# Gated linear attention and a cosine router: causal scores without their empty quarter, all masks on GpSimd

## The chip, the cores and the metric

The kernel runs on one core of a Trainium2 chip. The metric is the device time of one execution in microseconds (us). The core has a matrix engine (TensorE, in the profile PE, with its weight loads as PEld), a vector engine (VectorE, DVE), a scalar engine (ScalarE, ACT), a general engine (GpSimd, POOL) and an engine that issues transfers (SyncE, SP). Each runs its own instructions in order, and they wait for each other through semaphores. Sixteen DMA engines move data.

## The reference

Two blocks follow each other. The first is a recurrence with 4 batches, 8 heads, 768 positions and a head size of 48; its output is the input of a router with 8 experts of 1024 hidden units:

```python
for t in range(S):
    state = alpha[:, :, t, :, None] * state + np.einsum('bhd,bhe->bhde', k[:, :, t], v[:, :, t])
    y[:, :, t] = np.einsum('bhd,bhde->bhe', q[:, :, t], state)
...
x = np.ascontiguousarray(attn_out.transpose(0, 2, 1, 3)).reshape(B * S, H * D)
...
logits = xn @ en.T / tau
expert_idx = np.argmax(logits, axis=1)
...
    h = np.maximum(x[mask] @ w1[e], 0.0)
    out[mask] = gate_w[mask, None] * (h @ w2[e])
```

All data are fp32.

## The kernel before

**Stages.** The recurrence is computed in 24 chunks (`NS`) of 128 positions, six to a batch. Within a chunk it is an attention with decays: scores of all keys with all queries, masked so that a key acts on its own and later positions only, times `v`, and to it the queries times the state carried from the chunk before. Afterwards a routed expert stage runs over blocks of 128 tokens. The change touches the attention stage alone.

**A chunk.** Eight heads make four pairs (`NP = 4`); a pair's two heads, padded to 64, fill the 128 partitions. `decays` turns `alpha`, `k` and `q` on TensorE (`pa`, `pk`, `pq`), makes on VectorE the scan `r` and the keys `kr = pk * r` (L484). `queries` copies `pq` to `qc` on ScalarE; `decay_queries` makes the scan `a` on VectorE and the queries `qs = qc * a` on GpSimd (L510). `scores` makes for each pair, each half of the keys (64) and each head `hh` one product of 64 keys and 128 queries, each on a quarter of the array (64 rows by 64 columns), into one PSUM tile `sc` per `hh`. The mask is put on by VectorE for `hh = 0`, as a product with a triangle (L577); for `hh = 1` ScalarE copies the scores to SBUF (L578) and GpSimd's `affine_select` clears them (L579). `mix_states` puts queries times `dec` (the state with its decay, made on GpSimd, L535) into `pyx`; `mix_chunk` adds eight products of 128 keys and 128 queries (L617). `update` makes `pd` from the keys and `v`, and VectorE the new `state` (L560). `rows` turns `y` back to rows with the logits (`px`, `lg`, `x`).

**Order.** The loop over steps is a hand-written pipeline: step `s` makes decays and queries of chunk `s`, scores and masks of `s - 1`, `y` of `s - 2`, rows of `s - 3`. `in_turn` and `behind` order instructions behind named earlier ones (`issue_after`), so that each engine's queue has the order of the program:

```python
            if 0 <= s - 1 < NS:
                decay_state(s - 1)

                with in_turn(), tc.issue_after(st[s]["a_scan"].ins) if s < NS else ExitStack():
                    scores(s - 1)
```

**Transfers.** `load` issues the loads of a chunk on SyncE, two chunks ahead; four buffers each hold `alpha`, `k`, `q`, and five `v` (L455). When the tokens of a group of chunks have been routed (`choose`, `place`), their rows go to an HBM table `xs` by expert: `to_rows` (L311) is an indirect transfer of 128 rows of 393 floats, issued by GpSimd, here called a send. In the steps from the ninth on GpSimd issues one or two of them, behind the `qs` of the step. `fetch_early` (L181) loads the first rows of an expert on SyncE once the sends of the first 16 chunks have landed, and the first expert's weights (L141, L144) are issued behind it. In 15 steps GpSimd also clears a part of a later buffer (L784), and it keeps the running counts of the experts (L340).

Of the kernel before, what the change touches and what calls it, by code (L numbers as in the profile page):

```python
# [9 lines left out]
FP32 = mybir.dt.float32  # L10
I32 = mybir.dt.int32
AF = mybir.ActivationFunctionType
ALU = mybir.AluOpType
# [14 lines left out]
def kernel(  # L28
# [12 lines left out]
    nc = tc.nc  # L41
    B, H, S, D = q.shape
    E, DM = expert_emb.shape
    F = w1.shape[2]
    P = 128
    DP = 64
    NP = H // 2
    NCH = S // P
    N = B * S
    NS = N // P  # L50
# [4 lines left out]
    HALF = P // 2  # L55
# [18 lines left out]
    consts = ctx.enter_context(tc.tile_pool(name="consts", bufs=1))  # L74
# [1 line left out]

    ident = consts.tile([P, P], FP32)
    make_identity(nc, ident)
    causal = consts.tile([P, 1, P], FP32)
    earlier = consts.tile([P, P], FP32)  # L80
    ones = consts.tile([P, P], FP32)
    cols_i = consts.tile([P, E], I32)
# [4 lines left out]
    part = consts.tile([P, 1], FP32)  # L87
# [102 lines left out]
    def mm(*args, **kwargs):  # L190
        last["pe"] = nc.tensor.matmul(*args, **kwargs)  # L191
# [4 lines left out]
    def in_turn():  # L196
        return tc.issue_after(last["pe"].ins) if last else ExitStack()


    with ExitStack() as c1:  # L200
        keep = c1.enter_context(tc.tile_pool(name="keep", bufs=1))
        work = c1.enter_context(tc.tile_pool(name="work", bufs=2))
        ps_tr = c1.enter_context(tc.tile_pool(name="ps_tr", bufs=3, space=PSUM))
        ps_sc = c1.enter_context(tc.tile_pool(name="ps_sc", bufs=1, space=PSUM))
# [4 lines left out]
        NBUF, NBV = 4, 5  # L209
# [2 lines left out]
        kt_s = [keep.tile([P, H, DP], FP32, name=f"kt{i}") for i in range(NBUF)]  # L212
        vt_s = [keep.tile([P, H, DP], FP32, name=f"vt{i}") for i in range(NBV)]

        NR = 3
        r_s = [keep.tile([P, NP * P], FP32, name=f"r{i}") for i in range(NR)]

# [3 lines left out]
        def fixed_parts():  # L221
            for i in range(NBUF):
                nc.gpsimd.memset(at_s[i][:, :, D:DP], 1.0)

                nc.gpsimd.memset(at_s[i][0:1], 0.0)
                nc.vector.memset(kt_s[i][:, :, D:DP], 0.0)
                nc.vector.memset(qt_s[i][:, :, D:DP], 0.0)
                if i == 0:
                    nc.gpsimd.memset(inr, 0.0)
                    for p in range(NP - 1):  # L230
                        nc.gpsimd.memset(inr[:, p * P + P - 1 : (p + 1) * P], 1.0)
                    for j in range(NR):
                        nc.vector.memset(r_s[j][:, NP * P - 1 :], 1.0)
                if i < 2:
                    nc.vector.memset(ini_s[i], 0.0)
            make_upper_triangular(nc, causal[:, 0], val=1.0, diag=True)
            for i in range(NBV):
                nc.vector.memset(vt_s[i][:, :, D:DP], 0.0)

        chunk_of = "b h (c p) d -> b c p h d"  # L240
        a_r, q_r, k_r, v_r = (t.rearrange(chunk_of, p=P) for t in (alpha, q, k, v))
# [149 lines left out]
        def counts(n):  # L391
# [32 lines left out]
            nc.vector.tensor_tensor(used, bc(r, shp, 2), bc(starts, shp, 1), ALU.is_gt)  # L424
            return nc.vector.tensor_copy(used_i, used[0:1])

        st = [dict() for _ in range(NS)]
        carried = {}

        def turned(t, name):  # L430
            pt = ps_tr.tile([P, NP * P], FP32, tag="tr", name=name)
            with in_turn():
                for p in range(NP):
                    tr(
                        pt[:, p * P : (p + 1) * P],
                        t[:, 2 * p : 2 * p + 2].rearrange("p h d -> p (h d)"),
                        ident,
                    )
            return pt
# [4 lines left out]
        def load(s):  # L444

            if s < NS:
                b, c = divmod(s, NCH)
                i = s % NBUF
                for p0, p1 in ((1, AROW), (AROW, P)):
                    nc.sync.dma_start(out=at_s[i][p0:p1, :, 0:D], in_=a_r[b, c, p0:p1])  # L450
                nc.sync.dma_start(out=kt_s[i][:, :, 0:D], in_=k_r[b, c])
                nc.sync.dma_start(out=qt_s[i][:, :, 0:D], in_=q_r[b, c])
            if s > 0:
                b, c = divmod(s - 1, NCH)
                return nc.sync.dma_start(out=vt_s[(s - 1) % NBV][:, :, 0:D], in_=v_r[b, c])  # L455

        def behind(s):

# [5 lines left out]
        def decays(s):  # L464

            d = st[s]
            i = s % NBUF
            L = NP * P
            pa = turned(at_s[i], "pa")
            r = r_s[s % NR]
            nc.vector.tensor_tensor_scan(  # L477
                r[:, L - 2 :: -1], pa[:, L - 1 : 0 : -1], inr[:, L - 2 :: -1],
                1.0, ALU.mult, ALU.add,
            )  # L480
            pk = turned(kt_s[i], "pk")
            d["kr"] = kr = work.tile([P, NP, P], FP32, name="kr", bufs=3)
            krf = kr.rearrange("p n t -> p (n t)")
            nc.vector.tensor_tensor(krf, pk, r, ALU.mult)  # L484
            d["pq"] = turned(qt_s[i], "pq")
            d["a"] = pa, r

# [7 lines left out]
        def decay_queries(s):  # L495
            c = s % NCH
            d = st[s]
            L = NP * P
            pa, r = d["a"]
            rv = r.rearrange("p (n t) -> p n t", t=P)  # L500
            ini = ini_s[s % 2]
            nc.vector.reciprocal(
                ini.rearrange("p (n t) -> p n t", t=P)[:, :, 0:1], rv[:, :, 0:1]
            )
            a = work.tile([P, L], FP32, name="a")
            d["a_scan"] = by_dve = nc.vector.tensor_tensor_scan(  # L506
                a, pa, ini, 0.0, ALU.mult, ALU.add
            )
            d["qs"] = qs = work.tile([P, NP, P], FP32, name="qs", bufs=4)
            by_pool = nc.gpsimd.tensor_tensor(  # L510
                qs.rearrange("p n t -> p (n t)"), d["qc"], a, ALU.mult
            )
            if c > 0:
                d["end"] = end = work.tile([P, NP, 1], FP32, name="end", bufs=3)
                nc.gpsimd.tensor_tensor(end, rv[:, :, 0:1], al0[:, :, s : s + 1], ALU.mult)
            d["last"] = by_dve, by_pool
# [45 lines left out]
        def scores(s):  # L562

            d = st[s]
            kr, qs = d["kr"], d["qs"]
            d["sm"] = sm = [work.tile([P, NP, P], FP32, name=f"sm{hh}") for hh in range(2)]
            sc = [ps_sc.tile([P, NP, P], FP32, name=f"sc{hh}") for hh in range(2)]
            for p in range(NP):
                for i in range(2):
                    to = slice(i * HALF, (i + 1) * HALF)  # L570
                    for hh in range(2):
                        sl = slice(DP * hh, DP * hh + DP)
                        mm(
                            sc[hh][to, p], lhsT=kr[sl, p, to], rhs=qs[sl, p],
                            start=True, stop=True, skip_group_check=True,
                        )
            nc.vector.tensor_tensor(sm[0], sc[0], causal.to_broadcast([P, NP, P]), ALU.mult)  # L577
            nc.scalar.copy(sm[1], sc[1])  # L578
            d["masked"] = nc.gpsimd.affine_select(  # L579
                out=sm[1], in_=sm[1], pattern=[[0, NP], [1, P]], base=0,  # L580
                channel_multiplier=-1, compare_op=ALU.is_ge, fill=0.0,
            )

# [22 lines left out]
        def mix_chunk(s):  # L608

            d = st[s]  # L610
            pyx, sm, vt = d["pyx"], d["sm"], vt_s[s % NBV]
            d["yT"] = yT = [work.tile([P, NQ, P], FP32, name=f"ycols{hh}") for hh in range(2)]
            for hh in range(2):
                for p in range(NP):
                    q, to = p // 2, DP * (p % 2)
                    mm(
                        pyx[hh][to : to + DP, q * P : (q + 1) * P],  # L617
                        lhsT=vt[:, 2 * p + hh], rhs=sm[hh][:, p],
                        start=("dec" not in d and q == 0), stop=True, skip_group_check=True,
                    )  # L620
                nc.scalar.copy(yT[hh].rearrange("p q t -> p (q t)"), pyx[hh][:, 0:YX])

        def rows(s):
# [92 lines left out]
        for s in range(NS + 3):  # L716
# [9 lines left out]
            if s < NS:  # L726
                decays(s)
# [9 lines left out]
            if s < NS:  # L737
                queries(s, copied)
                decay_queries(s)
            if 0 <= s - 1 < NS:  # L740
                decay_state(s - 1)

                with in_turn(), tc.issue_after(st[s]["a_scan"].ins) if s < NS else ExitStack():
                    scores(s - 1)
            if s == 0:
                with behind(s), in_turn():
                    prepare_first(a0)
                with behind(s):
                    prepare_logits()
# [7 lines left out]
                    mix_chunk(s - 2)  # L757
            if 0 <= s - 1 < NS:

                with in_turn(), tc.issue_after(st[s]["a_scan"].ins) if s < NS else ExitStack():  # L760
                    update(s - 1)
            if 0 < s < NS and s % NCH == 0:

# [17 lines left out]
            if 4 <= s < 4 + NXG * (NC + 1):  # L781
                i, t = divmod(s - 4, NC + 1)
# [6 lines left out]
            if s >= NS:  # L789
                n = placing(s)  # L790
# [14 lines left out]
            for r in rows_of(s):  # L805
                g = group_of[r]
# [578 lines left out]
```

## Time and profile before

| what | value |
|---|---|
| median of 14 executions | 416.43 us (415.88 to 418.13) |
| the profiled execution | 418.62 us, its span 416.7 us |
| busy in the span: PE, PEld, DVE, ACT, POOL | 398.3, 353.6, 287.7, 195.0, 221.2 us |
| attention stage in the span | up to about 155 us |
| DMA packets of under 512 bytes | 102,287 of 119,379 |

How to read it: busy time is summed over the whole span, and the stages have different limits; the windows and the timeline show a stage by itself. "L579" is line 579 of the kernel before. In lines of the waits the three numbers are the total in us, how often, and the longest. In lines of the timeline the numbers are start and duration in us, and in brackets the idle time of the engine just before it and what ended it. A fp32 product appears as two records on PE.

### The profile page before, as it was taken

The page shows a single profiled execution, that of the slowest core. Times are in us where ns is not written, and L with a number is a line of the kernel's source. Part 1 is how long each engine was busy: PE and PEld are TensorE (multiplying, and loading weights), DVE is VectorE, ACT ScalarE, POOL GpSimd, SP SyncE. Part 2 cuts the span into 40 slices and gives each one's busy share as a digit, 9 for nine tenths or more (in the row PEclk, how much of TensorE's full clock was granted, in tenths as well). Part 3 has the DMA queues.
Part 4 walks back from the last instruction along what each step waited for, and adds up shares of the span by engine and source line. Part 5 has one row for each costly group of instructions (what it writes and reads, how often), then busy time and mean ns, then how long its engine had stood idle before and what let it go on. Part 6 is the DMA issues. An engine that isn't in the chain of part 4 may idle for free. (4 is left out here: it accounts for less than half of the span.)

```text
span 416.7 us, 12552 instructions
## 1 busy us (share of the span) xinstructions
PE 398.3 (96%) x4954; PEld 353.6 (85%) x4954; DVE 287.7 (69%) x634; ACT 195.0 (47%) x481; POOL 221.2 (53%) x288
## 2 busy tenths in 40 slices
PE   7999999999989899999999999999999999999994
PEld 6789979888879677678979989889979989979974
DVE  7898979699799515882596696692595379487530
ACT  4455544455435424553653643732651472662320
POOL 7546577767665436831762843932671482682001
PEclk9999999999999999999999999999999999999998
DMA  9999999999994893595703805604701900101001
GB/s 138 159 163 156 155 207 179 198 183 187 198 174 113 295 349 112 150 359 171 263 16 117 297 18 184 220 19 147 260 19 39 339 28 19 41 0 36 21 16 43
DMA packets 119379, 60.28 MB, mean 145 GB/s; under 512 B 102287, under 2 KB 113816, under 8 KB 119312
## 3 DMA queue, kind: packets, MB, share of 16 engines
q1 hardware_dynamic: 115208, 49.14, 49.5%
q0 software_dynamic: 3728, 10.16, 6.9%
q8 instruction: 46, 0.75, 0.8%
q14 instruction: 21, 0.17, 0.1%
q10 hardware_dynamic: 376, 0.05, 0.1%
HBM read 49.69 MB, written 11.45 MB: 147 GB/s over the span
## 5 line engine op out<-in xcount | busy, mean ns | idle before, releaser
L852 POOL DMA_INDIRECT out_dram<-y,sx x25 | 24.6, 982 | 103.4 <-DVE y L1161 42.3
L982 DVE TENSOR_TENSOR hT<-pq,hT 128x512 f32<-128x512 f32 x63 | 43.6, 692 | 46.2 <-PE pq L1082 44.4
L1082 PE MATMUL pq<-xT_m,w_m 128*128 128x128 f32 x560 | 67.2, 275 | 0.0
L1082 PEld LDWEIGHTS pq<-xT_m,w_m 128*128 128x128 f32 x560 | 64.7, 192 | 0.3 <-issue 0.3
L510 POOL TENSOR_TENSOR qs<-qc,a 128x512 f32<-128x512 f32 x24 | 30.6, 1276 | 37.0 <-DVE a L506 22.9
L1034 POOL TENSOR_TENSOR w_m<-w_m,w 128x512 f32<-128x512 f32 x30 | 43.2, 1446 | 1.4
L965 PE MATMUL pyo<-w,hT 128*128 128x384 f32 x128 | 42.6, 486 | 0.0
L1082 PE MATMUL pq<-xT_m,w 128*128 128x128 f32 x280 | 38.4, 277 | 0.6
L1082 PEld LDWEIGHTS pq<-xT_m,w 128*128 128x128 f32 x280 | 34.9, 192 | 2.1 <-issue 1.8
L987 ACT ACTIVATE hT<-hT 128x512 f32<-128x512 f32 x35 | 22.1, 631 | 31.2 <-DVE hT L982 31.2
L965 PEld LDWEIGHTS pyo<-w,hT 128*128 128x128 f32 x128 | 23.7, 190 | 14.8
L477 DVE TENSOR_TENSOR_SCAN r<-pa,inr 128x511 f32<-128x511 f32 x24 | 29.2, 1215 | 6.1 <-PE pa L194 5.9
L191 PE MATMUL sc<-qs,kr 64*64 64x128 f32 x768 | 29.6, 273 | 3.8 <-issue 3.8
L311 POOL DMA_INDIRECT xs<-x,dest x24 | 24.2, 1009 | 13.3 <-DVE x L653 8.4
L506 DVE TENSOR_TENSOR_SCAN a<-pa,ini 128x512 f32<-128x512 f32 x24 | 29.3, 1223 | 1.0
L1154 PE MATMUL pq<-w_m,hT_m 128*128 128x192 f32 x168 | 28.4, 326 | 0.0
L191 PEld LDWEIGHTS sc<-qs,kr 64*64 64x64 f32 x768 | 22.8, 133 | 6.2 <-issue 6.0
L1154 PEld LDWEIGHTS pq<-w_m,hT_m 128*128 128x128 f32 x168 | 27.5, 190 | 0.0
L191 PE MATMUL pyx<-sm,vt 128*64 128x128 f32 x384 | 26.3, 279 | 0.0
L649 ACT COPY lg<-pyx 128x32 f32<-128x32 f32 x24 | 4.4, 185 | 44.5 <-PE px L191 38.3
L191 PEld LDWEIGHTS pyx<-sm,vt 128*64 128x64 f32 x384 | 20.5, 136 | 4.3 <-issue 3.6
L1034 POOL TENSOR_TENSOR w_m<-w 128x512 f32<-128x512 f32 x12 | 15.3, 1274 | 15.9 <-PE pq L1082 15.9
(229 smaller groups left out, 917.7 us busy)
## 6 DMA issues: line engine op xcount, KB each, us to landing
w<-in_moe_w_dram SPq DMA_DIRECT2D x16, 1536.0 KB
kt<-in_k_dram SPq DMA_DIRECT2D x24, 192.0 KB
qt<-in_q_dram SPq DMA_DIRECT2D x24, 192.0 KB
vt<-in_v_dram SPq DMA_DIRECT2D x24, 192.0 KB
xg<-xs SPq DMA_DIRECT2D x22, 196.5 KB
at<-in_alpha_dram SPq DMA_DIRECT2D x24, 168.0 KB
xg<-xs SPq DMA_DIRECT2D x8, 98.2 KB
at<-in_alpha_dram SPq DMA_DIRECT2D x24, 22.5 KB
```

Of the source, the lines that this page charges most:

```text
L191: last["pe"] = nc.tensor.matmul(*args, **kwargs)
L311: ins = nc.gpsimd.indirect_dma_start(out=xs, out_offset=bass.IndirectOffsetOnAxis(ap=rows, axis=0), in_=x, in_offset=None, bounds_check=E ...
L477: nc.vector.tensor_tensor_scan(r[:, L - 2 :: -1], pa[:, L - 1 : 0 : -1], inr[:, L - 2 :: -1], 1.0, ALU.mult, ALU.add,)
L506: d["a_scan"] = by_dve = nc.vector.tensor_tensor_scan(a, pa, ini, 0.0, ALU.mult, ALU.add)
L510: by_pool = nc.gpsimd.tensor_tensor(qs.rearrange("p n t -> p (n t)"), d["qc"], a, ALU.mult)
L852: ins = nc.gpsimd.indirect_dma_start(out=out, out_offset=bass.IndirectOffsetOnAxis(ap=col, axis=0), in_=y, in_offset=None, bounds_check=N - 1,
L965: pe[:] = [nc.tensor.matmul(py, lhsT=hT[:, f], rhs=w2_t[:, f], start=(f == 0), stop=(f == FT - 1),)]
L982: dve[:] = [call(*args, **kwargs)]
L987: act[:] = [call(*args, **kwargs)]
L1034: by(to, x, y, op)
L1082: pe[:] = [nc.tensor.matmul(to[:, f], lhsT=left[:, f * P : (f + 1) * P], rhs=right, start=start and f == 0, stop=stop, skip_group_check=Tr ...
L1154: pe[:] = [nc.tensor.matmul(to, lhsT=left[:, f], rhs=right[:, f], start=start and f == 0, stop=stop and f == n - 1, skip_group_check=True,)]
```

## The change

The upper half of the queries is not multiplied with the lower half of the keys any more where the mask would clear all of it: of 16 products with 128 queries, eight keep 128 and eight have 64. The PSUM tiles of the scores become permanent and are set to zero once at the start, since a quarter of them is never written. For the pairs 2 and 3 the two key halves change places: `kr` is written with its halves swapped for them (two products on VectorE in place of one), and `v` of these heads is loaded with its halves swapped (three loads in place of one). So four products of equal size, one on each quarter of the array, stand next to each other. In `y`, the first 64 queries need the first 64 keys only: four products of 64 by 64 with 64 queries are split off, and of the eight others four have 64 queries.

The masks: ScalarE copies both score tiles to one SBUF tile, laid out so that the half-blocks that need the triangle lie at partitions 0 to 63 in its first half and at 64 to 127 in its second. GpSimd clears them in two `affine_select`, each on 64 partitions with 512 elements. VectorE's mask and its triangle are gone.

```diff
+        sc_s = [ps_sc.tile([P, 2, NP, HALF], FP32, name=f"sc{hh}") for hh in range(2)]
...
-            make_upper_triangular(nc, causal[:, 0], val=1.0, diag=True)
+            for sc in sc_s:
+                nc.vector.memset(sc, 0.0)
...
+        def part_of(i):
+            return slice(i * HALF, (i + 1) * HALF)
...
-                return nc.sync.dma_start(out=vt_s[(s - 1) % NBV][:, :, 0:D], in_=v_r[b, c])
+                vt = vt_s[(s - 1) % NBV]
+                nc.sync.dma_start(out=vt[:, 0:NP, 0:D], in_=v_r[b, c][:, 0:NP])
+                for i in range(2):
+                    last_v = nc.sync.dma_start(
+                        out=vt[part_of(i), NP:H, 0:D], in_=v_r[b, c][part_of(1 - i), NP:H]
+                    )
+                return last_v
...
-            krf = kr.rearrange("p n t -> p (n t)")
-            nc.vector.tensor_tensor(krf, pk, r, ALU.mult)
+            pkh, rh = (t.rearrange("p (n h t) -> p n h t", h=2, t=HALF) for t in (pk, r))
+            krh = kr.rearrange("p n (h t) -> p n h t", h=2)
+            nc.vector.tensor_tensor(krh[:, 0:2], pkh[:, 0:2], rh[:, 0:2], ALU.mult)
+            nc.vector.tensor_tensor(krh[:, 2:4, ::-1], pkh[:, 2:4], rh[:, 2:4], ALU.mult)
...
-            for p in range(NP):
-                for i in range(2):
-                    to = slice(i * HALF, (i + 1) * HALF)
+            for part in range(4):
+                j, kh = divmod(part, 2)
+                for g in range(2):
+                    p, to = 2 * g + j, part_of(kh ^ g)
                     for hh in range(2):
-                        sl = slice(DP * hh, DP * hh + DP)
+                        sl = part_of(hh)
+                        q2 = qs[sl, p].rearrange("d (h t) -> d h t", h=2)
+                        if kh:
+                            sc, q2 = sc_s[hh][to, 1 - g, p], q2[:, 1]
+                        else:
+                            sc, q2 = sc_s[hh][to, :, p], q2[:, ::-1] if g else q2
                         mm(
-                            sc[hh][to, p], lhsT=kr[sl, p, to], rhs=qs[sl, p],
+                            sc, lhsT=kr[sl, p, part_of(kh ^ g)], rhs=q2,
                             start=True, stop=True, skip_group_check=True,
                         )
-            nc.vector.tensor_tensor(sm[0], sc[0], causal.to_broadcast([P, NP, P]), ALU.mult)
-            nc.scalar.copy(sm[1], sc[1])
-            d["masked"] = nc.gpsimd.affine_select(
-                out=sm[1], in_=sm[1], pattern=[[0, NP], [1, P]], base=0,
-                channel_multiplier=-1, compare_op=ALU.is_ge, fill=0.0,
-            )
+
+        def masks(s):
+
+            sm = st[s]["sm"] = work.tile([P, 2, 2, NP, HALF], FP32, name="sm")
+            for hh in range(2):
+                nc.scalar.copy(sm[:, hh], sc_s[hh])
+            for i in range(2):
+                x = sm[part_of(i), :, i].rearrange("s a p t -> s a (p t)")
+                st[s]["masked"] = nc.gpsimd.affine_select(
+                    out=x, in_=x, pattern=[[0, 2], [0, NP], [1, HALF]], base=0,
+                    channel_multiplier=-1, compare_op=ALU.is_ge, fill=0.0,
+                )
...
+            for j in range(2):
+                for g in range(2):
+                    p = 2 * g + j
+                    mm(
+                        pyx[g][part_of(j), g * P : g * P + HALF],
+                        lhsT=vt[part_of(g), 2 * p + g], rhs=sm[part_of(g), g, g, p],
+                        start="dec" not in d, stop=True, skip_group_check=True,
+                    )
             for hh in range(2):
-                for p in range(NP):
-                    q, to = p // 2, DP * (p % 2)
-                    mm(
-                        pyx[hh][to : to + DP, q * P : (q + 1) * P],
-                        lhsT=vt[:, 2 * p + hh], rhs=sm[hh][:, p],
-                        start=("dec" not in d and q == 0), stop=True, skip_group_check=True,
-                    )
+                for g in range(2):
+                    for j in range(2):
+                        p = 2 * g + j
+                        if g == hh:
+                            first_at, x = HALF, sm[:, hh, 1 - g, p]
+                        else:
+                            first_at, x = 0, sm[:, hh, ::-1, p] if g else sm[:, hh, :, p]
+                        mm(
+                            pyx[hh][part_of(j), g * P + first_at : (g + 1) * P],
+                            lhsT=vt[:, 2 * p + hh], rhs=x,
+                            start=False, stop=True, skip_group_check=True,
+                        )
```

In the loop over steps `masks(s - 1)` is called behind `scores(s - 1)` under the same order.

More of the change, by code (lines that the diff above doesn't have):

```diff
@@ L78 @@
     make_identity(nc, ident)
-    causal = consts.tile([P, 1, P], FP32)
     earlier = consts.tile([P, P], FP32)
@@ L565, in scores @@
             kr, qs = d["kr"], d["qs"]
-            d["sm"] = sm = [work.tile([P, NP, P], FP32, name=f"sm{hh}") for hh in range(2)]
-            sc = [ps_sc.tile([P, NP, P], FP32, name=f"sc{hh}") for hh in range(2)]
-            for p in range(NP):
-                for i in range(2):
-                    to = slice(i * HALF, (i + 1) * HALF)
-                    for hh in range(2):
-                        sl = slice(DP * hh, DP * hh + DP)
+            for part in range(4):
+                j, kh = divmod(part, 2)
+                for g in range(2):
+                    p, to = 2 * g + j, part_of(kh ^ g)
+                    for hh in range(2):
+                        sl = part_of(hh)
[4 more added lines that the diff above has]
+                            sc, q2 = sc_s[hh][to, :, p], q2[:, ::-1] if g else q2
                         mm(
-                            sc[hh][to, p], lhsT=kr[sl, p, to], rhs=qs[sl, p],
+                            sc, lhsT=kr[sl, p, part_of(kh ^ g)], rhs=q2,
                             start=True, stop=True, skip_group_check=True,
                         )
-            nc.vector.tensor_tensor(sm[0], sc[0], causal.to_broadcast([P, NP, P]), ALU.mult)
-            nc.scalar.copy(sm[1], sc[1])
-            d["masked"] = nc.gpsimd.affine_select(
-                out=sm[1], in_=sm[1], pattern=[[0, NP], [1, P]], base=0,
-                channel_multiplier=-1, compare_op=ALU.is_ge, fill=0.0,
-            )
+        def masks(s):
[8 more added lines that the diff above has]
+                )
         NQ = NP // 2
@@ L739, with behind_scan @@
                 decay_queries(s)
+            def behind_scan():
+                return tc.issue_after(st[s]["a_scan"].ins) if s < NS else ExitStack()
             if 0 <= s - 1 < NS:
                 decay_state(s - 1)
-                with in_turn(), tc.issue_after(st[s]["a_scan"].ins) if s < NS else ExitStack():
+                with in_turn(), behind_scan():
                     scores(s - 1)
+                    masks(s - 1)
             if s == 0:
@@ L758 @@
             if 0 <= s - 1 < NS:
-                with in_turn(), tc.issue_after(st[s]["a_scan"].ins) if s < NS else ExitStack():
+                with in_turn(), behind_scan():
                     update(s - 1)
```

## The prediction

> **What bounds the kernel now.** I read the page first, then busy time by windows, then the timeline of GpSimd, then the waits.
>
> The page: the profiled execution took 418.62 us, of which 416.7 us are span, and it is 2.19 us above the median of 416.43 us. All terms below are differences against this trace; I add their sum to the median.
>
> ```profile
> PE   7999999999989899999999999999999999999994
> ...
> POOL 7546577767665436831762843932671482682001
> ...
> DMA  9999999999994893595703805604701900101001
> ```
>
> One digit is 10.4 us. The first 13 digits are the attention stage, the only one that the change touches. There TensorE and the DMA engines stand at 9, GpSimd at 5 to 7. The windows from 47 to 137 us say the same in microseconds:
>
> ```profile
> 47.00:92.00 45.00, 43.13 (x973) 38.19 (x972) 37.60 (x69) 22.75 (x71) 32.61 (x57) 1.00 1.01 190
> 92.00:137.00 45.00, 42.62 (x951) 38.50 (x954) 40.25 (x86) 21.67 (x67) 30.37 (x50) 1.00 0.86 170
> ```
>
> The columns are busy time of PE, weight load, DVE, ACT and POOL, then clock, DMA share and GB/s. PE is busy 95% of the time, POOL 70%. A step (one chunk of 128 positions) takes 5.7 us (the timeline has the transposes of `pa` at 25.56 and, 19 steps on, at 134.03 us: 108.5/19). So TensorE sets the pace of a step, and POOL idles about 1.6 us of it. Where, the timeline of GpSimd shows (two steps):
>
> ```profile
> 116.18 1.28 POOL L510 TENSOR_TENSOR qs<-qc,a 128x512 f32<-128x512 f32 x1 [1.87 <-DVE a L506]
> 117.61 1.04 POOL L311 DMA_INDIRECT xs<-x,dest  x1 [0.15 <-issue]
> 118.67 0.65 POOL L579 TENSOR_SCALAR_AFFINE_SELECT sm<-sm 128x512 f32<-128x512 f32 x1
> 119.27 0.62 POOL L535 TENSOR_TENSOR dec<-state,end 128x256 f32<-128x256 f32 x1
> 119.84 0.21 POOL L515 TENSOR_TENSOR end<-r,al 128x4 f32<-128x4 f32 x1
> 120.82 1.27 POOL L510 TENSOR_TENSOR qs<-qc,a 128x512 f32<-128x512 f32 x1 [0.77 <-ACT sm L578]
> ```
>
> The order to see: `qs`, then the send of a finished chunk's rows (`xs<-x`), then the mask, `dec`, `end`, and the next `qs`. POOL issues the send in 1.04 us and goes straight on; nothing on POOL waits for it to land. When it lands shows where SyncE waits for it (first the waits of SyncE's queue from 120 to 135 us, then the send):
>
> ```profile
> SPq L181 <- DMA xs<-x,dest: 7.2, 2, 5.1
> ```
>
> ```profile
> 129.48 1.01 POOL L311 DMA_INDIRECT xs<-x,dest  x1 [0.15 <-issue]
> ```
>
> **The change part by part.** I call a landing the time from the end of the send's issue to the last of its 16 completion steps in the trace's landing records. For the 16 sends of this stage it is 4.69, 3.61, 3.20, 2.92, 4.53, 3.80, 2.82, 2.71, 3.41, 4.27, 3.25, 3.23, 3.19, 3.95, 3.98 and 1.85 us (mean 3.46). The last one, after all input loads are in, is the shortest.
>
> *The new wait.* The built program's order on GpSimd, which may be read without running it, has in 12 steps:
>
> ```
> DMACopy xs<-x,dest
> TensorScalarAffineSelect sm<-sm 64x2x256 [waits Activation]
> TensorScalarAffineSelect sm<-sm 64x2x256 [waits DMASW0,Pool]
> TensorTensor dec<-state,end [waits DVE,Pool]
> TensorTensor end<-r_133,al_140 [waits DVE]
> TensorTensor qs<-qc,a [waits DVE,Activation]
> ```
>
> The second of the two selects waits for the counter of the send just issued, for its full value of 16, that is, for its landing. Before, the only select of a step waits for ScalarE alone. Queued behind this wait on POOL are `dec`, `end` and the next `qs`; `y` of the chunk (L617) waits for the mask, the state (L560) for `dec`, the next scores for `qs`. This decides the case, so here is the POOL time of the 12 steps (send positions 52.4 to 129.5 us before), one engine in order:
> - `qs` 1.28, first send 1.02, second select 0.64, handovers 0.15 + 2 x 0.07: 3.24 x 12 = 38.9. The first select lies inside the landing.
> - `dec` in 10 of them, 0.61: 6.1. `end` in 11, 0.21: 2.3.
> - four steps issue a second send, 0.97 and its gap: 1.2 x 4 = 4.8.
> - `xg` memset (L784) in six, 0.42: 2.5.
> - counts and token copies (L340, L810), 0.2 each, in four steps: 3.5.
> - landings: seven single sends under the loads, at the mean of the seven such rows (3.20, 2.92, 2.82, 2.71, 3.25, 3.95, 3.98: 3.26): 22.8. Two steps with two sends ahead of the select, at the second one's rows (4.27, 3.19: 3.73): 7.5. In the last three the loads run out, because steps get longer while the loads keep their pace; between 3.26 and 1.85 I take 2.55: 7.7. Sum 38.0.
>
> Together 58.1 + 38.0 = 96.1 us. A step with one send is about 4.4 + 3.26 = 7.7 us of POOL, 2 us over TensorE's step, so POOL sets the pace. TensorE does not come into this loop: `a` for the next `qs` follows from the previous `y` by `pd`, `pkb`, `pa` (2.4 us after the select) and the scans (3.6 us), some 2.4 us before POOL gets to that `qs`. Two steps in between have no send and go at 5.4. So 14 steps take 96.1 + 10.8 = 106.9 us. Before, the same 14 steps lie between the ends of two `qs` at 51.90 and 134.02: 82.1 us. Difference: +24.8.
>
> *Less TensorE work.* Scores: 16 products in four rounds of four, 0.88 us by the start of the next group, 0.22 a round. Two of the rounds get 64 columns. The nearest row is `pyx<-sel` with 56 columns, 0.12 a round: 0.20 saved. For `y`: four rounds of two at 0.22 become one round of four (0.12), two of 128 columns (0.44) and two of 64 (the rows of `pd`, 0.12 to 0.14): 0.80 to 0.84 against 0.92, so 0.1 saved with four more instructions. The bounds are 0 (if loading weights sets the round) and 0.33 a step; I take 0.28. On the 14 steps it buys nothing, because POOL sets the pace. In the first four steps `pa` follows its load by 1.5 to 2.8 us, so the loads hold it; five steps remain: -1.4.
>
> *The rest.* DVE loses the mask (0.68) and makes `kr` in two calls; by the 128x256 row of L560 (0.42) that is +0.15, so -0.5 a step, not on the path. ACT gains one copy of 128x512 (0.65) at 22.75/45 busy: so it idles 2.8 us of a step, which covers it; without that cover `kb`, and `pq` behind it, would come up to 0.65 later a step. POOL gains the second select, 0.64 (0.3 if half the partitions took half the time), counted above. SyncE issues two more loads a step, 0.39 each where the queue is free; bytes and packets are the same; covered by 4 to 12 us by which loads lead their use after step 4. At the start two memsets of 0.49 go to DVE, which idles from 4.0 to 5.8 us there: nothing.
>
> *The end.* The last send is late by 24.8 less its own step's excess of about 1.9: 22.9. Through `fetch_early` (L181) and the first weights (L141) it sets the stage after; `y` of the last chunks is late by about as much. 22.9 - 1.4 + 0.5 (the longer landing there) = 22 us. The experts' stage is unchanged.
>
> Prediction: 416.4 + 22 = 438.4 us; profiled 440.6.
>
> Against the landing rows stands a rule. The Trainium skill, "DMA: Bandwidth & Descriptors", section "Anatomy of one DMA — SWDGE (gpsimd) path", gives 2.0 us plus bytes over 436 GB/s; with 128 rows of 1572 B that is an estimate of 2.5 us, by which the landings would sum to 29.5 and the total to 430. The rows are longer, most of them under full DMA engines, and I keep them. The same page, "Rules for kernel authors", says to issue early, compute, and wait late; this change waits at once.
>
> **The rivals.**
> 1. *POOL's slack swallows the wait, and TensorE's saving counts: faster.* 20 steps x 0.28 = -5.6: 410.8 us. For it: POOL idles 1.6 us a step. Its point: a landing below 5.4 - 4.4 = 1.0 us. None of 16 rows is below 1.85. Chance 0.04.
> 2. *Landings get short, because sends no longer meet a full queue.* All at 1.85: 58.1 + 22.2 + 10.8 - 82.1 - 2 = +7: 423.4. Against it: the loads keep their pace until they lead by four buffers, near the end. Chance 0.1 (down to 428).
> 3. *The idle time of TensorE drops its clock.* Before, the windows have one such case: 1.21 us of work in 141 to 144 us, then 0.50 of the clock for 3.4 us. Such a drop costs 1.7 us of TensorE's time; one a step hides in the 2.4 us of slack, two a step give 12 x 1.0 = +12: 450. Chance 0.12.
> 4. *The change's stated aim is not reached even on TensorE*, rounds of 64 columns costing 0.22: +1.4, within the first case.
>
> The Trainium skill, "TensorE: Matmul & The Clock Gate", section "HAM oscillation — how this bites in real kernels", ties the drop to idle gaps over about 3.4 us. By that rule rival 3 would cost nothing; the row above dropped after a gap of 2 us, so I keep the rival.
>
> **How the numbers follow.** The first case has 0.74. The range: landings from 1.9 to 4.3 us in all 12 steps give +8 and +36, so 424 to 452 us; the upper end takes in rival 3. No change means within 0.2% (0.8 us, about what a measurement of this kernel can tell): 0.01, which is rival 1 with its gain lost elsewhere. The rest of rival 1 is faster, 0.03; all else is slower, 0.96.
>
> **What would show it.** On the profile after: POOL waiting at the select line for `xs<-x` some 2.5 us, 12 times; POOL's busy share lower per microsecond and TensorE's digits falling from 9 to 6 or 7 between 52 and 155 us; steps of 7 to 8.7 us there and about 5.4 in the two without a send; scores at 0.68 and `y` at 0.82 us. Wrong: no such wait; steps with sends below 6 us; or the added time lying behind the attention stage.

## The result and the profile after

The changed kernel takes 446.74 us (median of 10 runs, 441.14 to 450.55), the kernel before, run beside it, 416.64 us (47 runs). The ratio is 1.068, with a 95% interval of 1.065 to 1.071: 28 us slower. (Ratios here compare undisturbed runs, so a ratio need not be that of the two medians beside it.) The profiled execution took 454.61 us, its span is 452.9 us, 36.2 us above the profile of before. It is longer than all ten of these runs, 7.9 us above their median, so terms of a few microseconds that are read from this one profile need not hold for the others.

The page: the busy shares by slices, one digit 11.3 us.

```profile
PE   7899967798696799895999999999999999999993
...
POOL 6666657675572675672048266392293274492001
PEclk9999989978976899999899999999999999999998
DMA  9977888999554149759181190450640450100001
```

Where TensorE stood at 8 or 9 before, seven of the nine slices from the sixth to the fourteenth are at 6 to 8, and PEclk is no longer 9 throughout. The same two windows as before (busy time of PE, weight load, DVE, ACT, POOL; clock, DMA share, GB/s):

```profile
47.00:92.00 45.00, 35.00 (x792) 32.27 (x794) 24.55 (x50) 20.05 (x60) 28.71 (x46) 0.92 0.89 163
92.00:137.00 45.00, 37.20 (x756) 33.76 (x753) 24.98 (x54) 18.10 (x55) 27.07 (x44) 0.85 0.77 147
```

TensorE is busy 8 us less in the first window, and GpSimd is less busy too (28.71 against 32.61 us) although it has a second select to do. Nobody works more; someone waits. The timeline of GpSimd shows who, and for what:

```profile
126.03 1.02 POOL L313 DMA_INDIRECT xs<-x,dest  x1 [0.15 <-issue]
127.08 0.68 POOL L602 TENSOR_SCALAR_AFFINE_SELECT sm<-sm 64x512 f32<-64x512 f32 x1
129.29 0.67 POOL L602 TENSOR_SCALAR_AFFINE_SELECT sm<-sm 64x512 f32<-64x512 f32 x1 [1.53 <-DMA xs<-x,dest]
130.04 0.61 POOL L548 TENSOR_TENSOR dec<-state,end 128x256 f32<-128x256 f32 x1
```

The first select runs behind the send, the second stands until the send has landed, and `dec` follows it. The waits of GpSimd over the stretch, and the page's row of `y`:

```profile
POOL sm L602 <- DMA xs<-x,dest: 27.4, 10, 4.8
...
POOL sm L602 <- DVE turn_f L383: 2.6, 1, 2.6
...
POOL sm L602 <- DVE x L689: 2.3, 1, 2.3
```

```profile
L190 PE MATMUL pyx<-sm,vt 128*64 128x64 f32 (+2 forms) x576 | 33.7, 263 | 23.0 <-POOL sm L602 23.0
```

The last two lines of the waits are the same wait under another name (the program has it in 12 steps, and in these two another semaphore moved last): 32.3 us in 12 steps. Of this 23.0 us reach TensorE as idle time ahead of `y`. SyncE's wait for the sends ahead of `fetch_early`, in its queue from 130 to 170 us, lasts longer too (before: 7.2 us):

```profile
SPq L180 <- DMA xs<-x,dest: 10.4, 2, 6.2
```

I measure all kernels below over one stretch, the 14 steps of the prediction: between the ends of two `qs`, the ninth and the 23rd of 24. Times in us from each kernel's profile, one execution each; kernels that nothing slows or speeds up here (before, e3_twice, e7_vtwo, e11_vfull) lie between 82.0 and 82.8:

| kernel | ninth `qs` ends | stretch | ratio to before (95%) |
|---|---|---|---|
| before | 51.90 | 82.1 | 1 |
| changed | 53.80 | 112.3 | 1.068 (1.065 to 1.071) |
| e1_wide | 54.84 | 85.6 | 1.023 (1.017 to 1.029) |
| e2_halves | 52.54 | 113.2 | 1.070 (1.064 to 1.075) |
| e3_twice | 51.85 | 82.8 | 1.000 (0.998 to 1.003) |
| e4_busy | 54.83 | 108.6 | 1.082 (1.075 to 1.088) |
| e5_vthree | 53.62 | 87.3 | 1.012 (1.005 to 1.019) |
| e6_vone | 52.66 | 78.9 | not comparable |
| e7_vtwo | 52.11 | 82.0 | 1.000 (0.997 to 1.002) |
| e8_copy | 54.55 | 84.0 | 1.015 (1.011 to 1.019) |
| e9_share | 52.72 | 82.8 | 1.007 (1.005 to 1.009) |
| e10_kb | 53.52 | 85.1 | 1.018 (1.014 to 1.022) |
| e11_vfull | 51.92 | 82.1 | 1.002 (0.999 to 1.005) |
| e12_onchip | 63.79 | 101.7 | 1.089 (1.084 to 1.094) |

### The profile page after: what moved, and what is told of

It reads as the page before. It is cut to its first block, busy times and chain, and to the rows that moved or that the text cites. A ratio compares the mean times of both kernels' runs of the same rounds, so it can differ in the third digit from the quotient of the medians.

```text
span 452.9 us, 13088 instructions
## 1 busy us (share of the span) xinstructions
PE 407.1 (90%) x5146; PEld 363.6 (80%) x5146; DVE 275.9 (61%) x636; ACT 204.6 (45%) x505; POOL 236.1 (52%) x310
## 5 line engine op out<-in xcount | busy, mean ns | idle before, releaser
L190 PE MATMUL pyx<-sm,vt 128*64 128x64 f32 (+2 forms) x576 | 33.7, 263 | 23.0 <-POOL sm L602 23.0
L190 PEld LDWEIGHTS pyx<-sm,vt 128*64 128x64 f32 (+1 forms) x576 | 29.3, 148 | 26.2 <-POOL sm L602 24.2
L602 POOL TENSOR_SCALAR_AFFINE_SELECT sm<-sm 64x512 f32<-64x512 f32 x48 | 32.0, 668 | 33.7 <-DMA xs<-x,dest 27.4
L1026 ACT ACTIVATE hT<-hT 128x512 f32<-128x512 f32 x35 | 22.1, 631 | 31.2 <-DVE hT L1021 31.1
L657 ACT COPY ycols<-pyx 128x256 f32<-128x256 f32 x48 | 17.4, 413 | 29.9 <-PE pyx L190 25.5
L313 POOL DMA_INDIRECT xs<-x,dest x24 | 24.2, 1010 | 10.8 <-DVE x L689 5.9
L599 ACT COPY sm<-sc 128x512 f32<-128x512 f32 x48 | 26.9, 639 | 0.4 <-PE sc L190 0.2
```

Source lines behind the costliest of these rows:

```text
L599: nc.scalar.copy(sm[:, hh], sc_s[hh])
L602: st[s]["masked"] = nc.gpsimd.affine_select(out=x, in_=x, pattern=[[0, 2], [0, NP], [1, HALF]], base=0, channel_multiplier=-1, compare_op= ...
```

## The experiments

### The wait alone, taken away and put in

**e1_wide** leaves everything of the change in place but the partitions of the second select. The half-block that needs the triangle is still cleared; the partitions 0 to 63, now covered as well, keep everything because of the base.

```diff
-                x = sm[part_of(i), :, i].rearrange("s a p t -> s a (p t)")
+                x = sm[0 : P if i else HALF, :, i].rearrange("s a p t -> s a (p t)")
...
-                    out=x, in_=x, pattern=[[0, 2], [0, NP], [1, HALF]], base=0,
+                    out=x, in_=x, pattern=[[0, 2], [0, NP], [1, HALF]], base=HALF * i,
```

> The changed kernel, but its second select of a step covers all 128 partitions (base 64, so that partitions 0 to 63 keep everything); the result is the same, and in the built program no select waits for a send any more, only for ScalarE. Theory A (the landing wait in 12 steps is the whole loss): no idle time of GpSimd in front of the select put down to xs<-x; the 14 steps between the ends of qs number 8 and 22 take 78 to 82 us instead of 112.3; the time is 411 to 417 us. Rival B (the second select, the second ScalarE copy or the three loads of v cost the time): over 430 us. If TensorE's saving of 0.2 us a step reaches the end, about 411 us; if the loads hold the early steps, about 416.

Measured: 431.56 us, ratio 1.023; the stretch is 85.6 us. The timeline of GpSimd in this kernel, with the same send of two at once that cost the changed kernel 4.8 us:

```profile
117.09 0.97 POOL L313 DMA_INDIRECT xs<-x,dest  x1 [0.31 <-issue]
118.06 1.29 POOL L602 TENSOR_SCALAR_AFFINE_SELECT sm<-sm 64x512 f32<-64x512 f32 x2
119.33 0.20 POOL L342 TENSOR_TENSOR before<-before,chosen 128x8 f32<-128x8 f32 x1
```

Both selects follow the send without a gap. So the wait costs 26.7 us of the stretch (112.3 less 85.6). But the kernel is not as fast as I expected: without any wait for a send it is still 2.3% slower than before, and theory A is not the whole loss.

**e2_halves** does the opposite: the old kernel, with its one select in two.

```diff
-            d["masked"] = nc.gpsimd.affine_select(
-                out=sm[1], in_=sm[1], pattern=[[0, NP], [1, P]], base=0,
...
+            for i in range(2):
+                x = sm[1][i * HALF : (i + 1) * HALF]
+                d["masked"] = nc.gpsimd.affine_select(
+                    out=x, in_=x, pattern=[[0, NP], [1, P]], base=-HALF * i,
```

> The kernel before, with nothing changed but its one select of a step cut into two of 64 partitions with 512 elements each, the second on partitions 64 to 127; in the built program this second select waits for the sends, as in the changed kernel. TensorE, VectorE, ScalarE and the loads do what they did. Theory A: 12 waits of 2 to 5 us on GpSimd; by the sum of the prediction with the landings of the changed kernel, +22 to +28 us: 438 to 445 us. Rival B (the loss comes from the other parts of the change): under 425 us, that is 24 selects more at 0.65 us, mostly hidden.

Measured: 447.97 us, ratio 1.070, which is the loss of the whole change; the stretch is 113.2 us. The waits of GpSimd between 40 and 165 us:

```profile
POOL sm L581 <- DMA xs<-x,dest: 32.5, 11, 4.8
```

**e3_twice** has the same number of selects, but the second covers all partitions:

```diff
+            for n in (HALF, P):
+                x = sm[1][0:n]
                 d["masked"] = nc.gpsimd.affine_select(
-                out=sm[1], in_=sm[1], pattern=[[0, NP], [1, P]], base=0,
+                    out=x, in_=x, pattern=[[0, NP], [1, P]], base=0,
```

> The kernel before with a second select a step, but this one on partitions 0 to 63 first and then on all 128, so that GpSimd has the work of two selects and no wait for a send. Theory A: GpSimd idles 1.6 us of a step, and 0.65 us more work fits into it: 416 to 418 us. Rival B (GpSimd's load with the second select is what counts): 0.65 us in each of 20 steps, about 429 us. The difference between this kernel and the one with two halves is then the price of the wait alone.

Measured: 417.92 us, ratio 1.000. The windows of this kernel:

```profile
47.00:92.00 45.00, 43.45 (x974) 38.44 (x973) 37.79 (x68) 22.74 (x70) 37.70 (x65) 1.00 0.96 183
```

GpSimd is busy 37.70 us of 45 instead of 32.61, and TensorE still 43.45: the extra select fits into GpSimd's idle time. The difference of 0.07 between the two ratios is the wait alone. What brings it in is the partitions: in the built programs here a select on partitions 64 to 127 waits for the counters of the sends still under way, one that begins at partition 0 does not. In e1_wide and e3_twice it is again the second select of a step, and it does not wait.

### What is left without the wait: the loads

In e1_wide TensorE waits for loads (kt and qt: 3.8 us between 40 and 165 us), which it hardly did before. The change splits each chunk's `v` into three loads. **e5_vthree** does this alone, on the old kernel and without a swap:

```diff
+                nc.sync.dma_start(out=vt[:, 0:NP, 0:D], in_=v_r[b, c][:, 0:NP])
+                for i in range(2):
+                    half = slice(i * HALF, (i + 1) * HALF)
+                    last_v = nc.sync.dma_start(
+                        out=vt[half, NP:H, 0:D], in_=v_r[b, c][half, NP:H]
+                    )
```

> The kernel before, with nothing changed but that each chunk's v comes in three loads as in the changed kernel (four heads on 128 partitions, and twice four heads on 64 partitions; not swapped). Theory D, formed from the kernel with the wide select, which lost 10 us without any wait for a send: in the built program each load on SyncE waits for the landing of the load eight places earlier, so seven loads a step instead of five cut the work in flight from 1.6 to 1.1 steps, and the DMA share falls from 1.01 to about 0.8: 424 to 430 us. Rival E (the loads cost nothing, the 10 us come from the masks' second copy or from the order of the products): 416 to 418 us.

Measured: 424.65 us, ratio 1.012; the stretch is 87.3 us, and the ninth `qs` ends 1.7 us late. So the three loads cost 1.2 of the 2.3% that e1_wide kept, and all that it lost within the stretch. Behind the stretch e1_wide's profile is 9.3 us longer than before, that of e5_vthree 1.8. In both TensorE waits there for the first expert's weights (4.9 and 4.0 us, before not at all), and e1_wide has two spells of half clock there, 13.7 us together; what sets them off no run separates. **e6_vone** is e1_wide with `v` in one load again:

```diff
-                nc.sync.dma_start(out=vt[:, 0:NP, 0:D], in_=v_r[b, c][:, 0:NP])
-                for i in range(2):
-                    last_v = nc.sync.dma_start(
...
+                return nc.sync.dma_start(out=vt[:, :, 0:D], in_=v_r[b, c])
```

> The kernel with the wide select, and v in one load a step as before; the halves of v are then not swapped for heads 4 to 7, so this kernel's y is another one, and its time alone is read. Theory D: the DMA share from 20 to 92 us is back at 0.95 or more, TensorE's waits for kt and qt go, and what is left is TensorE's saving: 409 to 414 us. Rival E: 422 to 430 us as with three loads.

Its total (432.95 us) says nothing, since other `y` go to other experts; in the attention stage, where the work does not depend on the data (16 sends in the stretch, as before), the stretch takes 78.9 us, 6.7 us less than e1_wide and 3.2 us less than before. That is the change's saving with both losses away, from one profile.

Is it the number of loads, or their shape? **e7_vtwo** (two loads of four heads) and **e11_vfull** (three loads of four, two and two heads) cover all 128 partitions with each load; the edits of the one and the other:

```diff
+                nc.sync.dma_start(out=vt[:, 0:NP, 0:D], in_=v_r[b, c][:, 0:NP])
+                return nc.sync.dma_start(out=vt[:, NP:H, 0:D], in_=v_r[b, c][:, NP:H])
```

```diff
+                for h0, h1 in ((0, NP), (NP, NP + 2), (NP + 2, H)):
+                    last_v = nc.sync.dma_start(out=vt[:, h0:h1, 0:D], in_=v_r[b, c][:, h0:h1])
```

> The kernel before, with v in two loads of four heads each, both on all 128 partitions. Theory D (the number of loads in flight counts): six loads a step, 1.33 steps in flight, between five and seven: 418 to 424 us. If loads of 64 partitions are what is slow, and not their number: 416 to 418 us, as before.

> The kernel before, with each chunk's v in three loads that all cover 128 partitions (four, two and two heads). It tells apart what made three loads dear and two loads free: the number in flight (seven loads a step, the eighth load waits for the first) or the loads of 64 partitions. Theory D (number): 421 to 426 us, as with the two loads of 64 partitions. If the 64 partitions are the cause: 416 to 418 us.

Measured: 417.28 and 417.44 us, ratios 1.000 and 1.002. So theory D, which I had formed from the order of the loads in the program, fell, although its 424 to 430 us had held for e5_vthree: seven loads a step cost nothing that shows, if each covers 128 partitions. The same window of e11_vfull, then of e5_vthree, with as many loads, the same packets and bytes:

```profile
47.00:92.00 45.00, 43.13 (x974) 38.30 (x973) 37.66 (x68) 22.91 (x71) 32.42 (x57) 1.00 0.98 185
```

```profile
47.00:92.00 45.00, 40.09 (x874) 34.25 (x871) 34.09 (x62) 21.12 (x65) 29.67 (x48) 1.00 0.81 158
```

The share of busy DMA engines falls from 0.98 to 0.81 and the rate from 185 to 158 GB/s when two of the three loads cover 64 partitions. With the changed products it is the same: 0.85 and 163 in e1_wide, 0.99 and 183 in e6_vone, over the same window. Why the engines run empty with such loads the traces do not tell (they do not say which engine moved a packet); that stays open.

### The clock

In the changed kernel's profile TensorE's clock stood at half for 30.7 us of the stretch; before, for none of it. **e4_busy** fills the gaps with work:

```diff
+                for _ in range(REPEATS.get(s, 0)):
+                    with in_turn():
+                        mix_again(s - 2)
...
+        REPEATS = {s: 3 for s in (9, 10, 11, 13, 14, 15, *range(17, 23))}
```

> The changed kernel, and in the 12 steps with a wait the 16 products of queries and state are repeated three times ahead of the products with sm (same values written again): about 1.5 us more of TensorE's work a step, laid into the time in which TensorE waits for the mask. Theory C (TensorE's clock, which stood at half for 30.7 us of this stage, takes a share of the loss): with more work in the gaps the clock holds, the half-clock time falls under 15 us, and the time falls to 436 to 442 us in spite of the added work. If GpSimd's chain alone sets the pace: 445 to 449 us whatever the clock does. If TensorE is on the path with its work: 12 x 1.5 = 18 us more, about 464 us.

Measured: 452.47 us, ratio 1.082. In the stretch the half-clock time fell to 10.2 us, and the stretch by 3.7 us; the repeated products are 13.4 us more of TensorE's work, in ten of the steps (two steps have no `dec`). But the kernel as a whole became slower, not faster: Theory C's 436 to 442 us fell, so did the 464 us of added work on the path, and the time lies above the 445 to 449 us of GpSimd's chain alone as well. Of the 3.7 us, 2.9 are shorter landings: the 12 waits for sends sum to 29.5 us here and to 32.3 in the changed kernel. What is left for the clock, net of the added products, is 0.8 us. (e2_halves has 27.3 us of half clock in its stretch, with the same loss.)

### Attempts at a faster version

**e8_copy** keeps the short scores with `v` in one load: the halves of the keys change places in PSUM only, and the copy puts them back.

```diff
-                nc.scalar.copy(sm[:, hh], sc_s[hh])
+                sc = sc_s[hh].rearrange("s x p t -> s p x t")
+                nc.scalar.copy(sm[:, hh, 0:2], sc[:, 0:2])
+                for i in range(2):
+                    nc.scalar.copy(sm[part_of(i), hh, 2:4], sc[part_of(1 - i), 2:4])
```

> A version that keeps the saving in the scores and does without both losses: v in one load and kr in one product as before, the keys of pairs 2 and 3 change places only in the PSUM tile of the scores, and ScalarE's copy puts them back (three copies for each head half in place of one); masks as in the kernel with the wide select, y by eight products of 128 queries as before. Theories A and D: no wait for sends, loads as before, TensorE 0.19 us a step less in the scores over 20 steps: 411 to 414 us. If ScalarE's six copies a step (about 0.9 us more) get on the path: 417 to 425 us.

Measured: 423.89 us, ratio 1.015. TensorE's waits from 40 to 140 us say what holds it:

```profile
PE pq L193 <- ACT kb L532: 5.5, 8, 1.0
```

The copy `kb` stands in ScalarE's queue behind six copies of scores. Two ways to relieve ScalarE: VectorE takes two of the six (**e9_share**), or it takes `kb` (**e10_kb**):

```diff
-                    nc.scalar.copy(sm[part_of(i), hh, 2:4], sc[part_of(1 - i), 2:4])
+                    to, of = sm[part_of(i), hh, 2:4], sc[part_of(1 - i), 2:4]
+                    nc.scalar.copy(to, of) if hh else nc.vector.tensor_copy(to, of)
```

```diff
-            nc.scalar.copy(kb, pkb)
+            nc.vector.tensor_copy(kb, pkb)
```

> The version with v in one load and ScalarE's copies, but VectorE makes two of the six copies of a step (those of 64 partitions for the first head half). In the trace of the version before it, TensorE waited 7.2 us between 20 and 140 us for the copy kb behind the six copies, while VectorE idled 1.5 us of a step just then. If ScalarE's queue was what held that version (theory F): the waits for kb go, the qs of index 22 ends at 131 to 133 us and the time is 413 to 416 us. If a longer way from the scores to the mask holds it: 420 to 424 us as before.

> The same version, but VectorE makes the copy kb in place of ScalarE, and ScalarE keeps its six copies of sm. Theory F: ScalarE is relieved by 0.6 us a step, 414 to 418 us; but kb then stands in VectorE's queue next to two scans of 1.22 us, and where it has to wait for one, TensorE's next transposes do too: then 418 to 424 us.

Measured: 419.95 us (1.007) and 424.11 us (1.018). Theory F holds for the cause: the wait for `kb` is gone in e9_share. But its stretch, 82.8 us, only equals that of before, for now `px` waits 3.1 us for `state`, which stands in VectorE's queue behind the two copies; and in e10_kb `kb` waits for the scans, as the second half of its expectation said (TensorE waits 3.9 us for it at `pq` and 2.8 at `px`).

**e12_onchip** keeps all of the change's products and the wide select, loads `v` once, and lets VectorE make the swapped halves:

```diff
+        def swap_values(s):
+            for i in range(2):
+                nc.vector.tensor_copy(
+                    vs_s[s % 2][part_of(i), :, 0:D], vt_s[s % NBV][part_of(1 - i), NP:H, 0:D]
+                )
```

> The changed kernel without its two losses: the second select covers 128 partitions, v comes in one load of 128 partitions, and VectorE makes the swapped halves of heads 4 to 7 on the chip (two copies of 64 partitions with 192 elements a step, 0.2 to 0.35 us each; VectorE gave up the mask of 0.68 us). Scores and y are those of the changed kernel (the buffer of dec has two turns in place of three). If the wait for the sends and the loads of 64 partitions are all that the change loses (theories A and E'), the 14 steps take 79 to 81 us as with one unswapped load (78.9) and the time is 412 to 415 us, under the kernel before. If something else of the change costs time as well, or the two copies get in the way of VectorE's scans: 417 us or more.

Measured: 448.41 us beside 411.69 us for the kernel before on the same chip, ratio 1.089. From 40 to 140 us TensorE waits for these copies, and VectorE's timeline shows why:

```profile
PE pd L190 <- DVE vs L467: 15.2, 11, 2.0
```

```profile
55.36 0.26 DVE L467 COPY vs<-vt 64x192 f32<-64x192 f32 x1
55.95 1.27 DVE L467 COPY vs<-vt 64x192 f32<-64x192 f32 x1
```

```profile
55.48 1.27 POOL L529 TENSOR_TENSOR qs<-qc,a 128x512 f32<-128x512 f32 x1 [1.00 <-DVE a L525]
56.69 0.42 POOL L831 MEMSET xg<- 128x393 f32 x1
```

The first copy begins before `qs` and takes 0.26 us; the second begins inside it and ends 0.1 us after the memset behind it. I had priced the copies at 0.2 to 0.35 us; their mean is 0.75. So no version here beats the kernel before, and e12_onchip does not tell whether wait and loads are all of the loss. That rests on e6_vone's stretch.

## Why the prediction was right, and where its terms were off

Forecast 438.4 us (424 to 452), measured 446.74: the mechanism and the range hold, the size was 8 us too small by the medians. By its steps, in the profile (36.2 us more span, of which 30.2 in the stretch, 1.9 ahead of it, 4.1 behind it; forecast 24.8, -1.4 and -1.4):

- **The wait in 12 steps, with `dec`, `end` and `qs` queued behind it, is right**, and it is shown: it costs 26.7 us of the stretch when taken out of the changed kernel, 31.1 when put into the old one. What the text could not say is why the second select waits; e1_wide and e3_twice tie it to its partitions. The 12 steps with a send took 5.9 to 13.8 us (7 to 8.7 were expected), the two without 4.2 and 6.2 (5.4).
- **The landings were nearly right.** The 12 that a select waited for are 4.10, 2.89, 3.06, 3.37, 3.33, 3.16 and 2.12 us (22.0, forecast 22.8), 5.34 and 5.29 behind two sends at once (10.6, forecast 7.5), and 3.16, 1.65 and 1.73 at the end (6.5, forecast 7.7): 39.2 against 38.0. That the sum came out so close is in part luck, since the pairs erred one way, the others the other. In the same two steps the second of a pair landed after 5.35 and 4.78 us in e2_halves, but after 2.77 and 3.07 in e4_busy; what makes the difference no run shows. The Trainium skill's figure ("DMA: Bandwidth & Descriptors", "Anatomy of one DMA — SWDGE (gpsimd) path"), an estimate of 2.5 us a send, would have left 9 us out; the trace does not agree, it has 1.65 to 5.34.
- **GpSimd waits for more than the sum had.** This is the term that was mis-sized. The 12 steps with a send took 102.0 us, forecast 96.1. Of these, 39.2 are the landings, 1.2 more than forecast, and 4.6 are waits that "TensorE does not come into this loop" had put at nothing: 1.9 us for `a`, 1.3 at `end` for `r`, 0.9 for `top` and 0.5 for `qc`. The remainder, 58.2, is GpSimd's own work, forecast 58.1. (The two steps without a send took 10.4 us, forecast 10.8.) The two largest stand in one step, first in the changed kernel, then in the kernel before, where the wait for `a` follows in the line at 116.18 us that the prediction shows:

```profile
143.17 0.21 POOL L528 TENSOR_TENSOR end<-r,al 128x4 f32<-128x4 f32 x1 [1.28 <-DVE r L488]
145.44 1.27 POOL L523 TENSOR_TENSOR qs<-qc,a 128x512 f32<-128x512 f32 x1 [1.94 <-DVE a L519]
```

```profile
113.97 0.20 POOL L515 TENSOR_TENSOR end<-r,al 128x4 f32<-128x4 f32 x1 [1.29 <-DVE r L477]
```

So they could be read before the change: in that step, which has no `dec`, GpSimd waits for both scans. They are not the clock's doing: e1_wide, which has no half clock in its stretch, has 1.29 and 1.94 us there, and 1.03 for `top`.

- **"The two more loads are covered" is wrong.** They were priced at their issue alone, 0.39 us. Their shape lowers the rate of all loads, and alone they cost 1.2% (e5_vthree). In the changed kernel this is nearly hidden, since steps of 8 us leave the loads time: e2_halves, with the old loads, has the same stretch. It shows in the 1.9 us ahead of the stretch, where -1.4 was forecast.
- **TensorE's saving** was forecast at 0.28 us a step, and at nothing under the waits. Under them it is no more than 0.9 us in the stretch (113.2 in e2_halves against 112.3), about what profiles of the unslowed kernels differ by. Without wait and extra loads it is 0.23 (e6_vone: 3.2 us in 14 steps): the scores save 0.19 as forecast, from 0.88 to 0.69, but `y` with its products of state takes 1.43 instead of 1.47, not 0.1 less.
- **The second select and ScalarE's copy are covered**, as forecast (e3_twice; e6_vone, which has both).
- **Rival 1** had a second error in it: even if the wait were swallowed, the change would not have come to 410.8 us, but to e1_wide's 1.023.
- **Rival 2** did not come: only the last two of the 12 landings were below 2 us.
- **Rival 3** came true in part. Half-clock time rose to 30.7 us; the first such spell, at 61.2 us, begins after TensorE has idled 3.2 us (before, it was 1.79 us of idle time ahead of the drop at 144 us). It did not make the loss: work, landings and the waits above add up to GpSimd's 12 steps, and e4_busy, with a third of the half-clock time, still lost 26.4 us of the stretch.
- **The end.** 4.1 us more lie behind the stretch in this profile; e2_halves has none (282.6 us from there on, before 282.7). One spell of half clock at 214.8 us accounts for 1.7 us at most; the rest stays open.

## What to carry to other kernels

Before cutting an instruction into halves by partitions, read the built program for the waits of the second half: here a GpSimd select that began at partition 64 got a wait for the sends that GpSimd had issued ahead of it, and one that covered all partitions (with a base that keeps everything in the other half) took the same time and had no such wait. Whether other instructions get it too, no run shows. Keep loads on all 128 partitions where the DMA engines are near full (1.01 in the window before). And add up the new queue of the engine that takes over work, not its busy share: the engine with idle time was each time (ScalarE in e8_copy, VectorE in e9_share and e12_onchip) the next one that TensorE waited for.

## What the runs showed of the hardware that was not expected

- A select on 64 partitions takes as long as one on 128 with the same elements in each: 0.64 against 0.63 us in e3_twice, which has both.
- Loads of 64 partitions among loads of 128 lower the share of busy DMA engines from 0.98 to 0.81 with the same packets (e5_vthree, e11_vfull).
- Of two sends issued 1.3 us apart the second landed 5.34 and 5.29 us after its issue in the changed kernel, 3.19 to 4.27 before and 2.77 and 3.07 in e4_busy; the single ones that a select of the changed kernel waited for took 1.65 to 4.10 us.
- VectorE's copy from SBUF to SBUF waits when it begins inside an instruction of GpSimd (e12_onchip): the 24 that did so took 0.31 to 1.72 us, the 24 others 0.25 to 0.31. The Trainium skill, "SBUF — State Buffer", section "SBUF: two separate sides", describes this as an exclusive lock on a port shared by the two engines; the trace agrees for the copies. That GpSimd waits for VectorE in turn it does not show: `qs` takes 1.26 to 1.31 us in that kernel, whether or not a copy is running when it begins.
